# One group of sixteen chunks in place of four groups of four: the prefix sums of a gated linear-attention and convolution kernel

## The chip, the cores and the metric

The kernel runs on one core of one Trainium2 chip. The metric is the time of one execution on the device in microseconds (us). The core has five engines with queues of their own: TensorE (PE, matrix products; PEld are its weight loads), VectorE (DVE), ScalarE (ACT), GpSimd (POOL) and SyncE (SP, which issues DMA transfers). Each engine works through its queue in order and waits at an instruction until the semaphores that it names have been reached.

## The reference, cut to what matters

```python
g = sigmoid((x * gate_w).sum(-1, keepdims=True))
a = A_ref(x, wqkv, wo)          # linear attention, 16 heads of 28
b = B_ref(x, log_A, A_imag, C, log_dt, D_skip)
return g * a + (1 - g) * b

# A_ref: q, k, v = x @ wqkv; phi(t) = where(t > 0, t + 1, exp(t)) + 1e-6
#        kv = phi(k)^T v per head; z = sum of phi(k)
#        o = phi(q) kv / (phi(q) z + 1e-6); return o @ wo
# B_ref: K[d, l] = 2 Re sum_n C[d, n] exp(A[d, n] dt[d] l), l = 0..2047
#        y[t, d] = sum over l <= t of K[d, l] x[t - l, d];  return y + x * D_skip
```

x is 2048 positions by 448 features, all in fp32. Where a feature's K is flat over all lags to working precision, its convolution is K[d, 0] times the running sum of x over positions; the kernel finds out whether that holds for all features, and otherwise runs a general convolution behind the timed part (not run with these inputs).

## The kernel before, in words

Work goes by 16 chunks of 128 rows. A chunk c is loaded by SP (load_x) both turned and plain, with three tiles ahead; split_t and split_n split it into a high and a low part (ACT copies the high part, POOL subtracts, line 243), and skip (line 259, POOL) writes y[:, c] = x * D_skip. The main loop runs c from 2 to 13. An iteration projects k of chunk c + 1 and q of chunk c on PE (eleven products each, line 346), applies phi on ACT and DVE (k_feature, k_high, k_low, q_post), and adds eleven products into g, the product of phi(k) with x (do_g, line 422). Behind the loop come the last chunk, the small products of kv with wv and wo, and a last stage that goes over the chunks again: normalise q (norm_a to norm_d), turn it on PE (line 657), multiply (attend, line 683), and add og * y (final_b, line 688), which goes out by SP. The order of every queue is the order in which the program is written.

The running sums of x are made on the side of this. Chunks are in four groups of four: in group g, partition p holds positions 4p to 4p + 3 of the group's 512. For each group
- group_load fetches the four chunks once more into a home;
- running_a and running_b are two accumulating transfers on POOL's queue each, which turn the four chunks into running sums along a partition (lines 433 and 437);
- group_split splits the last of them, the totals, into high and low parts (ACT, then POOL);
- group_heads multiplies both by a strict lower triangle of ones on PE, a pair of products (line 448), which gives what comes from lower partitions;
- convolve (DVE, lines 453 and 454, two chunks at a time) adds that and multiplies by near, the row K[d, 0], which stands in a PSUM bank; the last row of the group goes to u by SP;
- group_add adds the home to y by an accumulating transfer (line 459). It is issued after the last skip of its group.

What one group leaves to the next is added in the last stage: inter (one product, line 749) and the gates, turned on PE (line 642) and laid into `rows` by 15 small transfers (phi), make extra rows of attend's last product (rc, tail).

Of the kernel before, what the change touches and what calls it, by code (L numbers as in the profile page):

```python
# [34 lines left out]
G = 4  # L35
SMALL = 2.0 ** -70
# [4 lines left out]
RX = DT + 3 * NC  # L41
# [3 lines left out]
UL = 32  # L45
UZ = 4 * UL
# [7 lines left out]
def general_conv(ctx: ExitStack, tc: tile.TileContext, ga, y, og, okc, both, gin_d, out):  # L54
# [80 lines left out]
    grouped = lambda t: t.rearrange("(g p r) d -> p g (r d)", p=P, r=G)  # L135
    ygr = yg.rearrange("p (g r) d -> p g (r d)", r=G)
    SP.dma_start(out=ygr, in_=grouped(nat))
# [4 lines left out]
    SP.dma_start(out=grouped(out), in_=ygr)  # L142
# [3 lines left out]
def gated_mix_kernel(ctx: ExitStack, tc: tile.TileContext, xin, wq_d, wvo_d, abc_d, ldt_d, dsk_d,  # L146
# [21 lines left out]
    wvo = const.tile([P, 2, J, D], F32, name="wvo")  # L168
    wv, wo = wvo[:, 0], wvo[:DJ, 1]
    ident, trir = both[:, 0], both[:, 1]  # L170
    cst = const.tile([P, DJ + RX + 1], F32, name="cst")
    mask, gcat, sel = cst[:DJ, :DJ], cst[:UZ, DJ:DJ + RX], cst[:, DJ + RX:]
    gcr = const.tile([UZ, RX], F32R, name="gcr")
    ones = const.tile([P, P], F32R, name="ones")
    rows = const.tile([P, S], F32, name="rows")
    dsk = rows[:, D:2 * D]
    near, side = [], []
    u = const.tile([UZ, D], F32, name="u")
# [8 lines left out]
    spare = const.tile([P, G, D], F32, name="spare")  # L187
    room = const.tile([P, 2 * NAT + 3 * D], F32, name="room")
# [10 lines left out]
    POOL.memset(rows[DT:RX, 2 * D:], 0.0)  # L199
    POOL.memset(u, 0.0)  # L200
# [12 lines left out]
    abc = [t[:DJ, o:o + 2 * J * N].rearrange("p (i j n) -> p i j n", i=2, j=J) for t, o in ((pf, 3 * J * N), (room, 0))]  # L213
# [72 lines left out]
    def s4d_prepare():  # L286
# [37 lines left out]
        near.append(o[:, :D])  # L324
        for j in range(J):
            PE.transpose(o[:, j * DJ:(j + 1) * DJ], pn[:, j:j + 1].to_broadcast([DJ, P]), ident[:DJ, :DJ])

# [96 lines left out]

    homes = (wvo[:, 1], pq[:, NC - G:], room[:, :G * D].rearrange("p (r d) -> p r d", r=G), spare)
    sums, heads = {}, {}

    def group_load(g):
        SP.dma_start(out=homes[g], in_=xin[g * G:(g + 1) * G, :, NAT:LO].rearrange("r p d -> p r d"))

    def running_a(g):
        w = homes[g]
        POOL.dma_start(out=w[:, 1::2], in_=w[:, 0::2], accum_op=ALU.add)

    def running_b(g):
        w = homes[g]
        POOL.dma_start(out=w[:, 2:], in_=w[:, 1:2].to_broadcast([P, 2, D]), accum_op=ALU.add)

    def group_split(g):
        w = sums[g] = tp.tile([P, 2, D], F32R, name="sums", tag="v0", bufs=1)  # L440
        ACT.copy(w[:, 0], homes[g][:, G - 1])
        low(POOL, w[:, 1], homes[g][:, G - 1], w[:, 0])

    def group_heads(g):
        o = heads[g] = ps.tile([P, 512], F32, name="v", tag="v0")[:, :D]
        w = sums.pop(g)
        for i in range(2):
            PE.matmul(o, lhsT=tri, rhs=w[:, i], start=i == 0, stop=i == 1)  # L448

    def convolve(c):  # L450
        g, i = c // G, c % G
        a, full = homes[g][:, i:i + 2], [P, 2, D]
        DVE.tensor_tensor(out=a, in0=a, in1=heads[g][:, None, :].to_broadcast(full), op=ALU.add)
        DVE.tensor_tensor(out=a, in0=a, in1=near[0][:, None, :].to_broadcast(full), op=ALU.mult)
        if i and g < NC // G - 1:
            SP.dma_start(out=u[g:UL + g + 1:UL, None], in_=homes[g][P - 1:P, G - 1:].to_broadcast([1, 2, D]))

    def group_add(g):
        POOL.dma_start(out=y[:, g * G:(g + 1) * G], in_=homes[g], accum_op=ALU.add)
# [52 lines left out]
    group_load(0)  # L512
    for c in range(2, NC - 2):
        if c + 3 < NC:
            load_x(c + 3)
        if c == 2:
            SP.dma_start(out=cst, in_=cst_d)
        if c in (5, 6):
            group_load(c - 3)
# [10 lines left out]
        if c == 6:  # L530
            running_b(1)
        if c in (6, 8):
            running_a(c // 2 - 1)
# [11 lines left out]
        if c == 6:  # L545
            convolve(0)
        qo = project(c, wqh, wql, D + 2, "q")
        q_post(c, qo)
        if c < 5:
            steps(2 if c == 4 else 1)  # L550
        if c == 4:
            ACT.copy(tri, trir)
            ACT.copy(gcr, gcat)
# [9 lines left out]
        if c in (7, 9, 11):  # L563
            group_heads(c // 2 - 2)
        if c < 4:
            skip(c - 1)
            skip(c + 2)
            (running_a, running_b)[c - 2](0)
        if c < 6:
            split_n(c + 2, c > 3)  # L570
        if c == 3:
            group_load(1)
        if c == 4:
            running_a(1)
        if c == 5:
            group_split(0)
        if c in (7, 9, 11, 13):
            group_add(c // 2 - 3)
        for j in {12: (0, 1), 13: (2, 3)}.get(c, ()):
            w = xn_p.tile([P, NX], F32R, name="wo", tag="n") if j < 2 else xp.tile([P, XC], F32R, name="wo", tag="xr")  # L580
            w = w[:DJ, :2 * D].rearrange("p (i d) -> p i d", i=2)
            woh.append(w[:, 0])
            wol.append(w[:, 1])
            ACT.copy(woh[j], wo[:, j])
            low(POOL, wol[j], wo[:, j], woh[j])
# [4 lines left out]
    rc = []  # L590
    pn, th, tl, pd, dn, dp = {}, {}, {}, {}, {}, []

    def norm_a(c):
        pd[c] = room[:, 2 * NAT + c % 3 * D:][:, :D]
        POOL.tensor_tensor(out=pd[c], in0=pq[:, c], in1=zb, op=ALU.mult)  # L595
# [19 lines left out]
    def norm_c(c):  # L615
        n = pn[c] = room[:, c % 2 * NAT:][:, :NAT].rearrange("p (j t) -> p j t", j=J)
# [12 lines left out]

    def phi(c):  # L630
        if 0 < c < NC:
            a = c - 1 if c < NC - 1 else 0
            i = DT + 3 * c
            SP.dma_start(out=rows[i:i + 3, c * P:(c + 1) * P], in_=phs[c // (NC - 1)][a:a + 1].bitcast(F32))

    phs = []

    def gates_a(a, b):
        return og[:, a:b]

    def gates_b(g, o):
        PE.transpose(o[:g.shape[1], :P], g, ident)

    def gates_c(n, o, tag):
        w = tp.tile([P, D], F32R, name="phs", tag=tag)[:n, :3 * P].rearrange("p (i t) -> p i t", i=3)
        phs.append(w)
        ACT.copy(w[:, 0:2], o[:n, None, :P].to_broadcast([n, 2, P]))
        return lambda: DVE.tensor_tensor(out=w[:, 2], in0=o[:n, :P], in1=w[:, 0].bitcast(F32), op=ALU.subtract)
# [18 lines left out]
    def tail(c):  # L667
        ACT.copy(tl[c][DT:RX, 3], rows[DT:RX, c * P:(c + 1) * P])
# [56 lines left out]
    for i in range(4):  # L725
# [5 lines left out]
        if i == 2:  # L731
            gates_b(gates_a(1, NC - 1), g[0])
# [255 lines left out]
```

## Time and profile before

| | |
|---|---|
| median of 3 timed runs | 170.21 us (170.1 to 170.28) |
| the profiled execution's own time | 170.16 us |
| its span, first to last instruction | 168.4 us |
| busy: PE, PEld | 163.2 us, 146.9 us |
| busy: DVE, ACT, POOL | 115.6 us, 107.6 us, 118.9 us |
| DMA queues q1 (SP's) and q0 (POOL's): share of 16 engines | 38.4%, 23.4% |

A row of the profile names a line of the kernel, an engine, an operation, the tile written and those read. A row of a timeline is the start in us from the span's start, the duration, then this name; in square brackets stands how long the engine was idle before, and what ended that. In the groups, after the count, come busy us, the mean ns of one, and idle time. Matmuls are pipelined, so their durations overlap. A row of waits is the waiting instruction, what released it, total us, times, and the longest. A row of stretches is the stretch, then for PE, PEld, DVE, ACT and POOL the busy us with the count, the clock granted to PE, the DMA share and GB/s.

### The profile page before, as it was taken

To read this page: it belongs to the slowest core of one execution; us is meant where nothing else is said; L and a number is where in the kernel's file an instruction comes from. 1 tells how busy PE (TensorE), PEld (TensorE's weight loads), DVE (VectorE), ACT (ScalarE), POOL (GpSimd) and SP (SyncE) were. 2 spreads that over 40 slices of the span, in tenths; PEclk is the share of its full clock that TensorE was granted. 3 is DMA by queue.
4 is the path that set the end of the run, shared out by engine and by line. 5 is a ranking of instruction groups with operands and counts; after the bars stand their busy time and mean duration, and the time that the engine had idled before them with its cause. 6 is when DMAs were issued, how large, how long until landed. Compare 5 with 4: busy or idle time off the path is not lost.

```text
span 168.4 us, 2703 instructions
## 1 busy us (share of the span) xinstructions
PE 163.2 (97%) x852; PEld 146.9 (87%) x852; DVE 115.6 (69%) x230; ACT 107.6 (64%) x245; POOL 118.9 (71%) x128
## 2 busy tenths in 40 slices
PE   6899999999999999999999999999999999999992
PEld 2698999999998999999999999989879999999991
DVE  0837745685844966767568567878988989997551
ACT  3688668898395694775856687564845564574541
POOL 6082589988948999757869479749786997953100
PEclk9999999999999999999999999999999999999999
DMA  5989999999992949998999800900121221221213
GB/s 158 414 314 315 282 291 337 276 246 216 396 277 44 176 110 256 224 236 256 318 233 258 172 4 0 218 2 1 28 47 55 112 110 59 109 92 73 111 58 113
DMA packets 11750, 29.45 MB, mean 175 GB/s; under 512 B 1331, under 2 KB 8198, under 8 KB 11510
## 3 DMA queue, kind: packets, MB, share of 16 engines
q1 hardware_dynamic: 8838, 21.81, 38.4%
q0 software_dynamic: 2752, 7.34, 23.4%
q8 instruction: 7, 0.11, 0.3%
q10 hardware_dynamic: 144, 0.11, 0.2%
q14 instruction: 9, 0.07, 0.1%
HBM read 17.93 MB, written 3.67 MB: 128 GB/s over the span
## 4 chain that ended last, share of the span: by engine, by line
PE 68%; ACT 10%; issue 3%; POOL 3%; DVE 1%; ACTq 0%; POOLq 0%
PE a L683 21%; PE q L346 13%; PE g L422 13%; PE k L346 9%; PE tr L657 4%; ACT y L300 2%; PE m L760 2%; PE v L346 1%; ACT xn L253 1%; ACT y L301 1%; ACT e L374 1%; PE v L448 1%; PE k L780 1%; PE tr L780 1%; ACT xt L247 1%
## 5 line engine op out<-in xcount | busy, mean ns | idle before, releaser
L683 PE MATMUL a<-wk,th 128*128 128x448 f32 (+1 forms) x170 | 36.8, 361 | 0.1
L422 PE MATMUL g<-pkh,xn 128*128 128x448 f32 x112 | 35.8, 364 | 0.0
L683 PEld LDWEIGHTS a<-wk,th 128*128 128x128 f32 x170 | 29.5, 189 | 2.3 <-issue 0.7
L346 PE MATMUL q<-wqh,xt 128*128 128x450 f32 x120 | 27.6, 367 | 0.0
L346 PE MATMUL k<-wk,xt 128*128 128x448 f32 x121 | 26.8, 366 | 0.4 <-ACT wk L469 0.4
L243 POOL TENSOR_TENSOR xn<-xr,xn 128x448 fp32r<-128x448 f32 x16 | 22.8, 1424 | 6.1 <-ACT xn L253 6.1
L243 POOL TENSOR_TENSOR xt<-xr,xt 128x512 fp32r<-128x512 f32 x14 | 21.4, 1526 | 7.2 <-ACT xt L247 7.2
L346 PEld LDWEIGHTS k<-wk,xt 128*128 128x128 f32 x121 | 22.6, 188 | 2.8 <-ACT wk L469 0.8
L346 PEld LDWEIGHTS q<-wqh,xt 128*128 128x128 f32 x120 | 22.5, 189 | 1.7
L422 PE MATMUL g<-pkl,xn 128*128 128x448 f32 x64 | 23.4, 366 | 0.0
L259 POOL TENSOR_TENSOR y<-xr,rows 128x448 f32<-128x448 f32 x16 | 23.2, 1456 | 0.0
L422 PEld LDWEIGHTS g<-pkh,xn 128*128 128x128 f32 x112 | 21.1, 188 | 2.2
L595 POOL TENSOR_TENSOR room<-pq,zb 128x448 f32<-128x448 f32 x16 | 18.5, 1165 | 3.8 <-issue 2.7
L620 POOL TENSOR_TENSOR room<-pq,den 128x336 f32<-128x336 f32 x16 | 12.2, 763 | 7.4 <-ACT den L609 4.0
L375 DVE SCALAR_TENSOR_TENSOR k<-k,e 128x448 f32<-128x448 f32 x11 | 7.0, 632 | 12.7 <-ACT e L374 12.7
L373 ACT ACTIVATE e<-k 128x448 f32<-128x448 f32 x11 | 6.0, 545 | 13.5 <-PE k L346 13.5
L688 DVE SCALAR_TENSOR_TENSOR ot<-y,og,a 128x448 f32<-128x448 f32 (+1 forms) x17 | 10.7, 629 | 5.4 <-PE a L683 5.4
L665 DVE TENSOR_TENSOR th<-tr,th 128x512 fp32r<-128x512 f32 x16 | 11.0, 690 | 2.6 <-ACT th L664 2.0
L664 ACT CAST th<-tr 128x512 fp32r<-128x512 f32 x16 | 9.4, 588 | 5.0 <-PE tr L657 4.8
L422 PEld LDWEIGHTS g<-pkl,xn 128*128 128x128 f32 x64 | 11.2, 174 | 1.2 <-DVE pkl L385 0.2
L694 ACT COPY pq<-a 128x448 f32<-128x448 f32 (+1 forms) x17 | 8.7, 516 | 5.0 <-DVE ot L688 5.0
L346 PE MATMUL v<-wk,xt 128*128 128x448 f32 x55 | 11.8, 362 | 0.0
(183 smaller groups left out, 316.6 us busy)
## 6 DMA issues: line engine op xcount, KB each, us to landing
xr<-in SPq DMA_DIRECT2D x15, 512.0 KB, 5.9
out<-ot SPq DMA_DIRECT2D x15, 224.0 KB, 1.9
pq<-in SPq DMA_DIRECT2D x2, 896.0 KB
room<-in SPq DMA_DIRECT2D x2, 896.0 KB
wvo<-in SPq DMA_DIRECT2D x2, 896.0 KB
y<-in SPq DMA_DIRECT2D x2, 480.0 KB
y<-in SPq DMA_DIRECT2D x2, 450.0 KB
wvo<-wvo POOLq DMA_DIRECT2D x2, 448.0 KB, 5.5
```

The lines of the kernel that those rows point to most:

```text
L243: eng.tensor_tensor(out=o, in0=r, in1=h.bitcast(F32), op=ALU.subtract)
L259: POOL.tensor_tensor(out=y[:, c], in0=plain[c][:, :D], in1=dsk, op=ALU.mult)
L346: PE.matmul(o[:, :n], lhsT=a, rhs=b, start=run.n == 1, stop=not seq)
L375: DVE.scalar_tensor_tensor(out=pks[c], in0=pks[c], scalar=1.0, in1=e, op0=ALU.add, op1=ALU.max)
L422: PE.matmul(g[i][:a.shape[1], :D], lhsT=a, rhs=b, start=c == 0 and n == 0, stop=c == NC - 1 and n == len(seq) - 1)
L595: POOL.tensor_tensor(out=pd[c], in0=pq[:, c], in1=zb, op=ALU.mult)
L620: POOL.tensor_tensor(out=n[:, :3, :DJ].rearrange("p j (h d) -> p j h d", h=4), in0=a, in1=r[:, :H - 4].rearrange("p (j h) -> p j h", j=3)[ ...
L664: ACT.copy(h, ov)
L665: DVE.tensor_tensor(out=l, in0=ov, in1=h.bitcast(F32), op=ALU.subtract)
L683: PE.matmul(a[:, lo:hi], lhsT=u_, rhs=w_[:, lo:hi], start=n == 0, stop=n == 10)
L688: DVE.scalar_tensor_tensor(out=ot[:, lo:hi], in0=y[:, c, lo:hi], scalar=og[:, c:c + 1], in1=a[:, lo:hi], op0=ALU.mult, op1=ALU.add)
L694: ACT.copy(pq[:, c, lo:hi], a[:, lo:hi])
```

## The change

All 16 chunks become one group: partition p holds positions 16p to 16p + 15, so the running sum along a partition goes over all chunks, and one pair of products with the triangle gives what comes from lower partitions. Two homes hold eight chunks each (wvo and room); half_load fetches four chunks at a time. running(c) keeps the sum in one PSUM bank: DVE adds chunk c to it (line 432 of the changed kernel) and writes near times the sum over the chunk's place in the home (line 433). A table gives the rows of each iteration: two in iteration 6, three each in 7 to 10, two in 11. near is copied to SBUF, which frees its bank, and the projections of k alternate between two banks from iteration 8. group_add (line 436) stays; group 0 goes in iteration 8, then 1 in 9, 2 in 11, 3 in 12. Groups 0 to 2 are issued behind all skips (line 251) of their rows; group 3, y[12:16], stands ahead of skip(14) and skip(15), which then write those two chunks' rows of y anew, so that what the transfer adds there is left out of the output. whole_split and whole_head (line 447) make the one pair in iteration 12, ACT copies its result to `over` in iteration 13, and four transfers (head_add, line 451) add that to y, a broadcast over four chunks each. The carry between groups, the gates' transposes, the rows they made and their transfers go. The loads of wo and wv are in halves, wo in iteration 10 and wv in 12; wo is split one iteration earlier.

```diff
+ROWS = {6: (0, 1), 7: (2, 3, 4), 8: (5, 6, 7), 9: (8, 9, 10), 10: (11, 12, 13), 11: (14, 15)}
...
+    def running(c):
+        if not c:
+            sums.append(ps.tile([P, 512], F32, name="r", tag="v0")[:, :D])
+            ACT.copy(sums[0], home(0))
+        else:
+            DVE.tensor_tensor(out=sums[0], in0=home(c), in1=sums[0], op=ALU.add)
+        DVE.tensor_tensor(out=home(c), in0=near, in1=sums[0], op=ALU.mult)
+
+    def group_add(g):
+        POOL.dma_start(out=y[:, g * G:(g + 1) * G], in_=homes[g // 2][:, g % 2 * G:][:, :G], accum_op=ALU.add)
+
+    def whole_split():
+        w = tp.tile([P, 2, D], F32R, name="sums", tag="v0", bufs=1)
+        sums[0] = w
+        ACT.copy(w[:, 0], home(NC - 1))
+        low(POOL, w[:, 1], home(NC - 1), w[:, 0])
+
+    def whole_head():
+        o = ps.tile([P, 512], F32, name="v", tag="v0")[:, :D]
         for i in range(2):
+            PE.matmul(o, lhsT=tri, rhs=sums[0][:, i], start=i == 0, stop=i == 1)
+        sums[0] = o
+
+    def head_add(g):
+        POOL.dma_start(out=y[:, g * G:(g + 1) * G], in_=over[:, None, :].to_broadcast([P, G, D]), accum_op=ALU.add)
...
         if c == 10:
-            SP.dma_start(out=wo, in_=wvo_d[:DJ, 1])
-        if c == 11:
-            SP.dma_start(out=wv, in_=wvo_d[:, 0])
-        ko = project(c + 1, wkh, wkl, D, "v1" if c in (2, 4) else "k")
-        if c == 6:
-            group_heads(0)
-        if c > 6:
-            convolve(2 * c - 12)
+            for j in (0, 2):
+                SP.dma_start(out=wo[:, j:j + 2], in_=wvo_d[:DJ, 1, j:j + 2])
+        if c == 12:
+            for j in (0, 2):
+                SP.dma_start(out=wv[:, j:j + 2], in_=wvo_d[:, 0, j:j + 2])
+        ko = project(c + 1, wkh, wkl, D, "v1" if c in (2, 4) or c > 6 and c % 2 == 0 else "k")
+        rows = list(ROWS.get(c, ()))
+        if c > 6 and rows:
+            running(rows.pop(0))
         split_t(c + 2)
...
             split_n(c + 2, False)
+        if c == 13:
+            ACT.copy(over, sums[0])
         k_feature(c + 1, ko)
-        if c in (7, 9, 11):
-            group_split(c // 2 - 2)
-        if c in (7, 9):
-            running_b(c // 2 - 1)
+        if c in (8, 9, 11, 12):
+            group_add((c - 7) * 2 // 3)
         if c > 5:
             skip(c + 2)
+        if c == 12:
+            whole_split()
         k_high(c + 1)
         k_low(c + 1)
...
-        if c in (7, 9, 11, 13):
-            group_add(c // 2 - 3)
...
+        for j in {11: (0, 1), 12: (2, 3)}.get(c, ()):
+            split_o(j)
+        if c == 12:
+            whole_head()
+        if c == 13:
+            for i in range(NC // G):
+                head_add(i)
...
-    carry = inter()
+    q_run(1)
     k1 = kv_products(1)
```

Where the instructions stand is best seen in the order itself. In POOL's queue before, these rows end iteration 12 and make up iteration 13: wo are the splits of wo, xt and xn those of chunk 15 (read from its tile xr_1002), y from xr is skip(15), and the DMA is group 3's transfer.

```order
L243 TENSOR_TENSOR wo_1063<-wvo_73,wo_1063 112x448 [waits DMAHW7_49,PE_49,Activation_49]
L243 TENSOR_TENSOR wo_1066<-wvo_73,wo_1066 112x448 [waits PE_49,Activation_49]
L243 TENSOR_TENSOR xt_1083<-xr_1002,xt_1083 128x512 [waits DMAHW3_49,Activation_49]
L243 TENSOR_TENSOR xn_1086<-xr_1002,xn_1086 128x448 [waits Activation_49]
L259 TENSOR_TENSOR y_59<-xr_1002,rows_77 128x448
L459 DMA y_59<-spare_86 128x1792 [waits DVE_49,Pool_49]
L243 TENSOR_TENSOR wo_1129<-wvo_73,wo_1129 112x448 [waits Activation_49]
L243 TENSOR_TENSOR wo_1132<-wvo_73,wo_1132 112x448 [waits Activation_49]
```

In the changed kernel the same queue from the end of iteration 11 to the end of 13: xr_921 is chunk 14, xr_991 chunk 15, sums is the low part of the totals, and DMASW3 is the semaphore of the fourth transfer that POOL issues, group 3's.

```order
L235 TENSOR_TENSOR wo_988<-wvo_73,wo_988 112x448 [waits PE_49,Activation_49]
L235 TENSOR_TENSOR xt_1007<-xr_921,xt_1007 128x512 [waits DMAHW7_49,Activation_49]
L235 TENSOR_TENSOR xn_1010<-xr_921,xn_1010 128x448 [waits Activation_49]
L436 DMA y_59<-room_84 128x1792 [waits DMAHW0_49,DVE_49,Pool_49]
L251 TENSOR_TENSOR y_59<-xr_921,dsk_76 128x448 [waits DMASW3_49]
L235 TENSOR_TENSOR sums_1019<-room_84,sums_1019 128x448 [waits Activation_49]
L235 TENSOR_TENSOR wo_1056<-wvo_73,wo_1056 112x448 [waits DMAHW6_49,Activation_49]
L235 TENSOR_TENSOR wo_1059<-wvo_73,wo_1059 112x448 [waits Activation_49]
L235 TENSOR_TENSOR xt_1077<-xr_991,xt_1077 128x512 [waits DMAHW0_49,Activation_49]
L235 TENSOR_TENSOR xn_1080<-xr_991,xn_1080 128x448 [waits Activation_49]
L251 TENSOR_TENSOR y_59<-xr_991,dsk_76 128x448
```

Group 3's transfer has moved from behind skip(15) to ahead of skip(14), and skip(14) names the semaphore of that transfer; the split of the totals stands behind it.

On PE, in the changed kernel, the end of g in iteration 12 and the start of iteration 13 (v from sums and tri is the pair with the triangle, k the projection of chunk 14):

```order
L414 MATMUL g_142<-pkl,xn 64x448
L414 MATMUL g_142<-pkh,xn 128x448
L447 MATMUL v<-sums,tri 128x448 [waits Activation_49]
L447 MATMUL v<-sums,tri 128x448 [waits Pool_49]
L338 MATMUL k<-wk_70,xt 128x448 x11
L338 MATMUL q<-wqh,xt 128x450 [waits DVE_49]
```

Before, iteration 13 follows on g of iteration 12 with nothing between; the four pairs stand behind k of iteration 6 and behind g of iterations 7, 9 and 11:

```order
L422 MATMUL g_145<-pkl,xn 64x448
L422 MATMUL g_145<-pkh,xn 128x448
L346 MATMUL k<-wk_70,xt 128x448 [waits DVE_49,Activation_49]
L346 MATMUL k<-wk_70,xt 128x448 [waits Pool_49]
L346 MATMUL k<-wk_70,xt 128x448 x9
```

So of four pairs one is left, one iteration later than the last of them was, and its second product waits for POOL.

More of the change, by code (lines that the diff above doesn't have):

```diff
@@ L439, in group_split @@
[L439 to L446, printed above, removed]
-        for i in range(2):
[L448 to L456, printed above, removed]
@@ L458, in group_add, with half_load, home @@
-    def group_add(g):
-        POOL.dma_start(out=y[:, g * G:(g + 1) * G], in_=homes[g], accum_op=ALU.add)
+    homes = (wvo, room)
+    sums = []
+    def half_load(h, i):
+        SP.dma_start(out=homes[h][:, i * G:(i + 1) * G],
+                     in_=xin[(2 * h + i) * G:(2 * h + i + 1) * G, :, NAT:LO].rearrange("r p d -> p r d"))
+    def home(c):
+        return homes[c // (2 * G)][:, c % (2 * G)]
+    def running(c):
[5 more added lines that the diff above has]
+        DVE.tensor_tensor(out=home(c), in0=near, in1=sums[0], op=ALU.mult)
@@ L696, in gated_mix_kernel @@
     c = NC - 2
-    POOL.memset(rows[DT:RX, D:2 * D], 0.0)
     gate(0, c)
     ko = project(c + 1, wkh, wkl, D, "v1")
-    uw = xt_p.tile([P, 2 * NAT], F32R, name="uw", tag="t")[:UZ, :D]
     k_feature(c + 1, ko)
-    ACT.copy(uw, u)
-    low(POOL, uw[UL:2 * UL], u[UL:2 * UL], uw[UL:2 * UL])
     k_high(c + 1)
@@ L720, in gated_mix_kernel @@
     gate(c, c + 1)
-    POOL.memset(rows[DT:RX, :D], 0.0)
     norm_bd(0)
```

155 lines of the change are left out of this document (36 added, 119 removed).

## The prediction

> **What bounds the kernel now.** I read the page first: the span, TensorE's (PE's) row, and the clock digits.
>
> ```profile
> span 168.4 us, 2703 instructions
> PE 163.2 (97%) x852; PEld 146.9 (87%) x852; DVE 115.6 (69%) x230; ACT 107.6 (64%) x245; POOL 118.9 (71%) x128
> PEclk9999999999999999999999999999999999999999
> ```
>
> The program ran 170.16 us in the profiled execution, so 1.76 us lie around the span; the median of the three timed runs is 170.21 us, and I work against 170.16. PE is full and at full clock. The waits of PE's matmuls say whether it is ever held up; this is the whole list.
>
> ```profile
> PE q L265 <- POOL warm L197: 1.3, 1, 1.3
> PE k L346 <- ACT wk L469: 0.4, 1, 0.4
> ```
>
> Both lie in the first 6 us. From there to its last matmul at 165.2 us PE does not stand still, so the span is PE's list of matmuls, and other engines count only where they make PE wait. The chain of waits in order of time gives the pace and the triangle products.
>
> ```profile
> 63.02 0.41 PE v L448 x2
> 76.73 0.41 PE v L448 x2
> 90.45 0.41 PE v L448 x2
> 90.85 2.21 PE k L346 x11
> 97.47 2.20 PE k L346 x11
> ```
>
> Eleven products take 2.2 us, 0.20 us each: a row's "mean ns of one" (361 to 367) overlaps its neighbours, and a removed product is worth its distance to the next one. An iteration of the loop (k, q, g) takes 97.47 - 90.85 = 6.62 us.
>
> **What leaves PE.** The first pair, and the stretch behind the last g products, stand in PE's timeline.
>
> ```profile
> 50.94 0.96 PE L448 MATMUL v<-sums,tri 128*128 128x448 f32 x2
> 51.74 1.59 PE L346 MATMUL q<-wqh,xt 128*128 128x450 f32 x7
> ...
> 113.10 0.37 PE L422 MATMUL g<-pkh,xn 128*128 128x448 f32 x1
> 113.30 0.27 PE L642 MATMUL g<-both,og 128*14 128x128 f32 x1
> ...
> 113.61 0.36 PE L422 MATMUL g<-pkh,xn 128*128 128x448 f32 x1
> 113.81 0.37 PE L749 MATMUL z<-uw,gcr 128*112 128x448 f32 x1
> 114.02 1.81 PE L780 MATMUL k<-gs,wvo 128*112 128x112 f32 x16
> ```
>
> Four pairs go: 51.74 - 50.94 = 0.80, and 3 x 0.41 = 1.23. The carry's product (L749) goes: 114.02 - 113.81 = 0.21. Between 113.10 and 113.61 lie two g products (0.40) and the gates' transpose, so that is worth 0.11; its twin in the last stage (c = 9 there) counts the same. Together 2.46 us. One pair comes back: 0.41. The last product of each row of output changes its operands, not its shape's cost (112 against 128 rows of weights), and q_run(1) only moves one product earlier. PE's list becomes 2.05 us shorter. That is the whole gain, if nothing new waits.
>
> **What the change makes wait.** In the changed order of GpSimd (POOL), iteration 12 has group 3's accumulating transfer onto y[12:16] ahead of skip(14), which writes y[14]. So skip(14) waits for that transfer to land, and behind it on POOL stand the low part of the totals (which the new pair's second product needs), two wo splits, xt and xn of chunk 15, skip(15) and the four new transfers. In the kernel before, each such transfer stands behind the last skip of its group, and nothing in POOL's queue waits for it. When is it issued, and when does PE come to the pair? Before, iteration 13 has the order on ACT and POOL that iteration 12 has now: two wo splits, xt, xn.
>
> ```profile
> 87.99 1.17 POOL L243 TENSOR_TENSOR sums<-spare,sums 128x448 fp32r<-128x448 f32 x1 [1.49 <-ACT sums L441]
> 89.11 1.16 POOL L259 TENSOR_TENSOR y<-xr,rows 128x448 f32<-128x448 f32 x1
> ...
> 97.75 2.29 POOL L243 TENSOR_TENSOR wo<-wvo,wo 112x448 fp32r<-112x448 f32 x2 [3.13 <-ACT wo L584]
> 100.01 1.29 POOL L243 TENSOR_TENSOR xt<-xr,xt 128x512 fp32r<-128x512 f32 x1
> 101.27 1.15 POOL L243 TENSOR_TENSOR xn<-xr,xn 128x448 fp32r<-128x448 f32 x1
> 102.38 1.15 POOL L259 TENSOR_TENSOR y<-xr,rows 128x448 f32<-128x448 f32 x1
> 103.83 0.87 POOL L459 DMA_DIRECT2D y<-spare  x1 [0.30 <-POOL y L259]
> ```
>
> There k starts at 97.47 and the instruction behind xn at 102.38, 4.91 us later. In the changed kernel k of iteration 12 starts at 90.85 - 2.03 = 88.82 (four pairs earlier in the list are gone), so the transfer is issued at 88.82 + 4.91 = 93.73. How long does it take? The DMA issues give the microseconds from issue to landing.
>
> ```profile
> y<-wvo POOLq DMA_DIRECT2D x1, 896.0 KB, 10.4
> y<-pq POOLq DMA_DIRECT2D x1, 896.0 KB, 13.2
> y<-room POOLq DMA_DIRECT2D x1, 896.0 KB, 7.0
> y<-spare POOLq DMA_DIRECT2D x1, 896.0 KB, 6.5
> ```
>
> The two long ones ran beside loads and running-sum transfers; the last, issued at 103.83, had the engines to itself. In the changed kernel all chunks of x and both halves of wv can be in by 93, since they no longer queue on SP behind the row copies into u. I take 6.5, nearest to y<-spare; 10.4 and 13.2 are the upper end. It lands at 100.23. Then skip(14), 1.16, and the low part, 1.17: 102.56, and the second product of the pair can go at 102.6. PE finishes g of iteration 12 at 97.47 - 2.03 = 95.44 and the pair's first product at 95.64. **PE stands still for 102.6 - 95.64 = 7.0 us**; nothing covers it, because k of chunk 14 is behind the pair in PE's queue.
>
> A still PE may also lose its clock. The stretches after PE's last matmul, and the first weight loads of the run, bear on that.
>
> ```profile
> 164.92 0.27 PE L683 MATMUL a<-rc,th 112*128 112x224 f32 x1
> ```
>
> ```profile
> 167.75:168.00 0.25, 0.00 (x0) 0.00 (x0) 0.00 (x0) 0.00 (x0) 0.00 (x0) 0.62 0.09 33
> 168.00:168.40 0.40, 0.00 (x0) 0.00 (x0) 0.00 (x0) 0.00 (x0) 0.00 (x0) 0.50 0.00 0
> ```
>
> ```profile
> 1.33 0.13 PEld L265 LDWEIGHTS <-warm 128*128 128x128 bf16 x2 [1.33 <-POOL warm L197]
> 1.74 0.15 PEld L265 LDWEIGHTS <-warm 128*128 128x128 bf16 x1 [0.28 <-issue]
> ...
> 3.44 0.15 PEld L265 LDWEIGHTS <-warm 128*128 128x128 bf16 x1 [0.28 <-issue]
> 3.87 0.58 PEld L265 LDWEIGHTS <-warm 128*128 128x128 bf16 x3 [0.28 <-issue]
> ```
>
> The granted clock (the column after the five engines) is a half by 168.00; 0.62 over the quarter before puts the fall at about 167.8, 2.6 us after the last matmul ended at 165.19. An idle of 7.0 us is well past that. At the start, products of 512 columns come 0.43 us apart from 1.33 to 3.87, against 0.20 x 512/448 = 0.23 at full pace, then close up: about 2.6 us at half pace, 1.3 us lost (the clock digits do not show that start; the spacing does). I add 1.3; its ends are 0 (clock kept) and 2.6 (twice as long at half pace).
>
> The Trainium skill, "TensorE: Matmul & The Clock Gate", Part 1, says that after an idle window of about 3.4 us the array runs at half rate until it has been busy for about 3.4 us, and its closing table asks for no gaps over about 3 us. By that the loss would be an estimated 1.7 us and the sum 176.8; the trace here shows 2.6 for both times, and I go by the trace.
>
> **Parts that I cost at nothing.** VectorE (DVE): an iteration now has up to three rows of add and multiply, through PSUM.
>
> ```profile
> L375 DVE SCALAR_TENSOR_TENSOR k<-k,e 128x448 f32<-128x448 f32 x11 | 7.0, 632 | 12.7 <-ACT e L374 12.7
> L385 DVE SCALAR_TENSOR_TENSOR pkl<-k,pkh 128x448 fp32r<-128x448 f32 x11 | 6.8, 617 | 1.8 <-ACT pkh L379 1.8
> L665 DVE TENSOR_TENSOR th<-tr,th 128x512 fp32r<-128x512 f32 x16 | 11.0, 690 | 2.6 <-ACT th L664 2.0
> L454 DVE TENSOR_TENSOR room<-room,p 128x896 f32<-128x896 f32 x2 | 2.2, 1087 | 0.1
> ```
>
> Four other operations of 448 columns an iteration take 4 x 0.62 = 2.5 us, and two of 896 took 2.2: 4.7. Now it is 2.5 + 6 x 0.62 = 6.2 of 6.62 in iterations 7 to 10. It fits by 0.4; at 0.69 an operation (the 512-column row, the upper end) it is 6.6 and still fits. PE is covered by the 4.4 us (two times eleven products) between the end of one q and the start of the next, in which DVE has to read q's one bank, and k's banks now alternate. A gain is excluded: PE never waited for DVE.
>
> POOL loses eight running-sum transfers, four memsets and four small splits; ACT loses the copies of the gates' rows; SP loses the copies into u and rows. PE waited for none of them but in the first pair's 0.80, counted above. The wo halves now wait on SP for group 0's landing, with x of chunks 14 and 15 and wv behind them: k of iteration 8 starts at 63.02 + 0.41 - 1.21 = 62.2 now, the transfer is issued within 4.9 of that and landed by 77.5 (10.4), some 10 us ahead of iteration 12, which splits chunk 14. The four broadcast transfers are issued after skip(15), at about 102.6 + 2.3 + 1.3 + 1.15 + 1.15 = 108.5.
>
> ```profile
> 125.46 0.68 DVE L688 SCALAR_TENSOR_TENSOR ot<-y,og,a 128x448 f32<-128x448 f32 x1 [0.38 <-PE a L683]
> ```
>
> y is first read at 125.46 before, near 131 now; the first transfer is in by 122 even at 13.2, and rows 4, 8 and 12 are each read more than 10 us after the ones before them. The output rows have the same length and only lie farther apart; I see no reason for a change there.
>
> **Sum:** 170.16 - 2.05 + 7.0 + 1.3 = **176.4 us**.
>
> **Rivals.**
> *No wait on PE (faster).* If the transfer has landed, and the low part is done, when PE reaches the pair, only the 2.05 remain: 168.1. It decides at 95.6: the issue would have to be 7 us earlier, at 86.7, before xt of chunk 14 is split, or the landing nearly immediate. The order speaks against it; for it only that a wait in the order need not be long. 0.08.
> *A longer landing.* With other transfers still running, 10.4 in place of 6.5: 176.4 + 3.9 = 180.3. Group 2's transfer, issued within 4.9 us of k of iteration 11 (88.82 - 6.62 = 82.2), could still run. 0.10.
> *The clock stays.* The fall after 2.6 us is seen only at the end of the program: 175.1. 0.07.
> *VectorE becomes the bound.* If PSUM rows cost more, at 0.4 us over an iteration, times four: 178.1. 0.03.
>
> **How the numbers follow.** My forecast has 0.72. The low end: landing, issue and clock each half a microsecond kinder, 174.9, which takes in the kept clock. The high end: a landing of 8.7, the middle between 7.0 and 10.4, and a longer half pace, 176.4 + 2.2 + 0.6 = 179.2, which takes in the VectorE case. Outside lie 168.1 and 180.3, 0.18 together. Differences under 0.2% (0.34 us) are about what a measurement of this kernel can tell from none; faster has the first rival's 0.08, within 0.2% 0.01, slower 0.91.
>
> **What would show it.** In the changed profile: POOL's y row (skip) with a wait of about 6.5 us on the transfer y<-room; PE's second v product idle about 7 us, released by POOL's sums; a fall of the clock near 98 and products 0.4 us apart behind the pair; no other wait of PE. It is wrong if PE reaches k of chunk 14 near 96, if the transfer takes over 9 us, or if PE waits in iterations 7 to 10.

## The result: 6% slower, beyond the forecast, and the profile after

The changed kernel takes 180.51 us at the median of four executions (180.12 to 180.88), the kernel before 170.20: a ratio of 1.0606 [1.0582, 1.063]. The forecast was 176.4 us, 174.9 to 179.2: the direction is right, the time lies above the range. The profiled execution took 180.88 us, 1.88 of them around its span. (Of the four executions of "late head transfers" below, two, of 184.38 and 185.4 us, are marked slow, and its times are given from the other two.)

The page of the changed kernel: span, PE's row and the clock digits.

```profile
span 179.0 us, 2610 instructions
PE 165.3 (92%) x843; PEld 148.1 (83%) x843; DVE 112.8 (63%) x242; ACT 100.6 (56%) x223; POOL 106.9 (60%) x116
PEclk9999999999999999999999858999999999999999
```

PE is no longer full, and three slices have lost clock (8, 5 and 8). PE's waits (total us, times, longest; the third and last of the list is the old one at the start):

```profile
PE v L447 <- POOL sums L235: 6.6, 1, 6.6
PE a L650 <- DMA wk<-shl: 1.9, 1, 1.9
```

The first was forecast, the second was not. First POOL's timeline of the changed kernel around the pair, then PE's:

```profile
94.26 0.85 POOL L436 DMA_DIRECT2D y<-room  x1
100.68 1.12 POOL L251 TENSOR_TENSOR y<-xr,dsk 128x448 f32<-128x448 f32 x1 [5.57 <-DMA y<-room]
101.77 1.12 POOL L235 TENSOR_TENSOR sums<-room,sums 128x448 fp32r<-128x448 f32 x1
...
108.45 5.17 POOL L451 DMA_DIRECT2D y<-over  x4
```

```profile
96.02 0.37 PE L447 MATMUL v<-sums,tri 128*128 128x448 f32 x1
102.94 0.74 PE L447 MATMUL v<-sums,tri 128*128 128x448 f32 x1 [6.55 <-POOL sums L235]
103.47 4.31 PE L338 MATMUL k<-wk,xt 128*128 128x448 f32 x11
```

That is the chain of the prediction, step for step: transfer, skip(14) behind it, the low part of the totals, the pair's second product. Behind it eleven products take 4.3 us (4.11 in the chain of waits). The stretches there, with the granted clock in the third column from the end:

```profile
101.00:102.00 1.00, 0.00 (x0) 0.00 (x0) 0.00 (x0) 0.00 (x0) 1.00 (x2) 0.78 0.00 0
102.00:103.00 1.00, 0.06 (x1) 0.06 (x1) 0.00 (x0) 0.00 (x0) 1.00 (x2) 0.50 0.00 0
...
107.00:108.00 1.00, 1.00 (x5) 0.87 (x4) 0.00 (x0) 0.18 (x1) 1.00 (x2) 0.50 0.00 0
108.00:109.00 1.00, 1.00 (x6) 0.91 (x5) 0.00 (x0) 0.95 (x2) 1.00 (x2) 0.80 0.00 0
```

0.78 over a microsecond is 0.44 of it at a half: the clock falls at 101.56. In the same way it is back at 108.40. It was at a half for 6.84 us, and PE worked in the last 5.46 of these.

The chain of waits of the changed kernel goes on to the new wait:

```profile
110.38 2.21 PE g L414 x11
...
127.94 4.81 DMA wk<-shl
132.89 2.47 PE a L650 x11
...
170.42 4.69 PE a L650 x33
175.13 0.46 DVE ot L655
```

wk<-shl are the four small transfers by SP that finish the weights of attend. From issue to landing the one that the profile before has a time for took 2.9 us; now the one that is waited for takes 4.8. What shared the DMA engines with them is seen in the landing times of the transfers y<-over, and in stretches of 5 to 6 us (the last two columns are the share of the DMA engines and GB/s):

```profile
DMA to landing us min/median/max: 7.9/14.2/20.6
```

```profile
115.00:120.00 5.00, 5.00 (x26) 4.43 (x25) 3.07 (x6) 2.80 (x7) 0.00 (x0) 1.00 1.13 186
...
125.00:131.00 6.00, 5.96 (x38) 5.06 (x36) 4.94 (x13) 3.69 (x9) 4.68 (x6) 1.00 1.08 183
```

The four transfers of totals, issued from 108.5 on, fill all DMA engines from about 110 to 131, through the very stretch in which attend's weights are finished. In the kernel before they stood idle at that place:

```profile
115.00:120.00 5.00, 5.00 (x40) 4.58 (x39) 4.44 (x15) 2.48 (x6) 5.00 (x7) 1.00 0.02 5
```

The account, from the positions of the same products in the two profiled executions (us):

| step | forecast | measured, and from what |
|---|---|---|
| products saved up to the pair | -2.03 | -1.45: 96.02 against 97.47 |
| the new pair itself | +0.41 | +0.41, taken at full pace |
| wait at the pair | +7.0 | +6.72: 102.94 - 96.02 - 0.20 |
| half clock behind it | +1.3 | +2.75: from 102.94 to g at 110.38 are 7.44, at full pace 0.20 + 2.23 + 2.26 |
| wait for wk<-shl | 0 | +1.93 |
| the rest of PE's list, up to its last products | -0.43 | -0.45: 170.42 - 160.51 less the rows above |
| from the start of PE's last products to the end of the span | 0 | +0.69: 179.0 - 170.42 against 168.4 - 160.51 |
| around the span | 0 | +0.12 |
| together | +6.25 | +10.72 |

### The profile page after: what moved, and what is told of

Its sections match the earlier page's. It is cut to its first block, busy times and chain, and to the rows that moved or that the text cites. A ratio compares the mean times of both kernels' runs of the same rounds, so it can differ in the third digit from the quotient of the medians.

```text
span 179.0 us, 2610 instructions
## 1 busy us (share of the span) xinstructions
PE 165.3 (92%) x843; PEld 148.1 (83%) x843; DVE 112.8 (63%) x242; ACT 100.6 (56%) x223; POOL 106.9 (60%) x116
## 4 chain that ended last, share of the span: by engine, by line
PE 72%; issue 7%; DVE 6%; POOL 6%; ACT 3%; DMA 3%; ACTq 0%; POOLq 0%; DVEq 0%
PE a L650 20%; PE g L414 14%; PE q L338 13%; PE k L338 10%; PE v L338 9%; PE tr L627 3%; DMA wk<-shl 3%; PE q L257 3%; POOL xn L235 1%; POOL xt L235 1%; DVE r L432 1%; POOL y L436 1%; POOL y L251 1%; DVE den L590 1%; DVE room L433 1%
## 5 line engine op out<-in xcount | busy, mean ns | idle before, releaser
L650 PE MATMUL a<-wk,th 128*128 128x448 f32 (+1 forms) x187 | 39.5, 360 | 1.9 <-DMA wk<-shl 1.9
L650 PEld LDWEIGHTS a<-wk,th 128*128 128x128 f32 x187 | 32.5, 189 | 4.1 <-issue 2.1
L235 POOL TENSOR_TENSOR xt<-xr,xt 128x512 fp32r<-128x512 f32 x14 | 18.1, 1295 | 20.2 <-ACT xt L239 20.2
L235 POOL TENSOR_TENSOR xn<-xr,xn 128x448 fp32r<-128x448 f32 x16 | 18.6, 1161 | 10.1 <-ACT xn L245 10.1
L251 POOL TENSOR_TENSOR y<-xr,dsk 128x448 f32<-128x448 f32 x16 | 19.3, 1214 | 5.6 <-DMA y<-room 5.6
L338 PE MATMUL k<-wk,xt 128*128 128x448 f32 x88 | 22.1, 399 | 0.0
L338 PEld LDWEIGHTS k<-wk,xt 128*128 128x128 f32 x88 | 18.2, 207 | 1.9 <-ACT wk L461 0.5
L338 PE MATMUL v<-wk,xt 128*128 128x448 f32 x88 | 19.1, 364 | 0.0
L338 PEld LDWEIGHTS v<-wk,xt 128*128 128x128 f32 x88 | 16.5, 188 | 1.3
L338 PE MATMUL q<-wql,xt 128*128 128x450 f32 x45 | 11.9, 368 | 0.0
```

Of the source, the lines that this page charges most:

```text
L235: eng.tensor_tensor(out=o, in0=r, in1=h.bitcast(F32), op=ALU.subtract)
L251: POOL.tensor_tensor(out=y[:, c], in0=plain[c][:, :D], in1=dsk, op=ALU.mult)
L338: PE.matmul(o[:, :n], lhsT=a, rhs=b, start=run.n == 1, stop=not seq)
L650: PE.matmul(a[:, lo:hi], lhsT=u_, rhs=w_[:, lo:hi], start=n == 0, stop=n == 10)
```

## The theories

**A:** the order of POOL's queue makes the wait at the pair and the half clock behind it (about 9.5 us), and the transfers of totals, put where small transfers are due, make the rest. **Rivals:** that the clock is no loss of its own (the wait alone costs, and what is lost behind it would be lost anyway); that the totals' transfers cost wherever they are put, so that the change is dear even without the wait; that the saving of products is smaller because of the change itself (its running sums on VectorE) and not because of something beside it.

## Experiments on the wait and the clock

**The totals' transfers taken away.** The output lacks the totals of the lower partitions.

```diff
-        if c == 13:
-            for i in range(NC // G):
-                head_add(i)
```

> The changed kernel without the four broadcast transfers (what the totals give to y is left out); group 3's transfer still ahead of skip(14). Theory (two costs, each of its own): the pair waits 6.7 us and runs on at half clock for 2.6, and nothing waits for the wk rows or the outputs, 170.2 - 1.5 + 9.3 = 178.0. Rival (the wait at the pair costs nothing by itself, since the wk rows set the end anyway): 170 or less.

Measured: 178.97 us, ratio 1.0525 [1.0493, 1.0557]. The only wait of PE's matmuls in this kernel behind the start:

```profile
PE v L447 <- POOL sums L235: 6.6, 1, 6.6
```

The wait for wk<-shl is gone with the transfers, the pair's wait and the 4.11 us of the eleven products behind it stay. The time is now inside the range of the prediction. So the larger part of the loss belongs to POOL's order, and the second wait to the transfers.

**The same with the totals' split ahead of the transfer.** Only one row of POOL's queue moves; the totals' transfers are left out here too.

```diff
+        if c == 12:
+            whole_split()
         if c in (8, 9, 11, 12):
             group_add((c - 7) * 2 // 3)
...
-        if c == 12:
-            whole_split()
```

> Left out are the four transfers of totals, as in the run that took 178.97 us at the median, with which this one is to be compared; the one edit is that the split of the totals stands ahead of group 3's transfer and of skip(14) in POOL's queue. If the 6.6 us and the half clock behind it came from the split's place in the queue, the pair goes through without a wait, and the wait moves to the next product that needs what stands behind skip(14): v of chunk 15, which needs xt of chunk 15. skip(14) still ends about 6.4 + 1.1 us behind the transfer's issue near 95.4, then two wo splits (2.2) and xt (1.3): xt is ready near 106.4, and PE comes to v near 103.3, so it waits about 3.1 us. Time: 178.97 - 6.6 - 2.75 (half clock) + 3.1 = 172.7 if the clock stays. Rival on the clock: in the runs so far the clock stayed at a half for 6.8, 6.8 and 10.2 us, multiples of 3.4, as if it was judged in stretches of 3.4 us; a gap of 3.1 us can then still empty most of one such stretch, and up to 2.7 us are lost: 173.5 to 175.4.

Measured: 175.35 us, ratio 1.0293 [1.0223, 1.0363]. PE's waits, PE's timeline at the new wait, and the first and last stretch below full clock:

```profile
PE v L338 <- POOL xt L235: 3.9, 1, 3.9
```

```profile
103.17 0.37 PE L338 MATMUL v<-wk,xt 128*128 128x448 f32 x1
107.43 3.85 PE L338 MATMUL v<-wk,xt 128*128 128x448 f32 x10 [3.90 <-POOL xt L235]
```

```profile
107.60:108.00 0.40, 0.40 (x2) 0.38 (x3) 0.40 (x1) 0.00 (x0) 0.40 (x1) 0.64 0.00 0
110.80:111.20 0.40, 0.40 (x3) 0.35 (x2) 0.00 (x0) 0.00 (x0) 0.00 (x0) 0.60 0.00 0
```

The pair goes through, and what else stands behind skip(14) is late instead: xt of chunk 15. The wait is 3.9 us in place of 3.1, since the transfer took 7.4 us in place of 6.4. The clock did fall, as the rival had it, at 107.71, when PE had already been at work again for 0.3 us, and came back at 111.12: 3.41 us at a half, 1.7 lost. 178.97 - 6.6 - 2.75 + 3.9 + 1.7 = 175.2 accounts for the 175.35. The split's place is the cause of the pair's wait; but the transfer ahead of skip(14) holds up whatever is behind.

**PE kept at work while it waits.** Thirty-two idle products into a spare bank between the two of the pair.

```diff
-        for i in range(2):
-            PE.matmul(o, lhsT=tri, rhs=sums[0][:, i], start=i == 0, stop=i == 1)
+        PE.matmul(o, lhsT=tri, rhs=sums[0][:, 0], start=True, stop=False)
+        spin = ps.tile([P, 512], F32, name="spin", tag="k")
+        for i in range(32):
+            PE.matmul(spin[:, :D], lhsT=tri, rhs=sums[0][:, 0], start=True, stop=True)
+        PE.matmul(o, lhsT=tri, rhs=sums[0][:, 1], start=False, stop=True)
```

> The changed kernel with 32 idle products of 448 columns between the first and the second product of the pair (they add work that the output does not use). Theory (the half pace behind the wait is the clock, and the clock falls for lack of work): PE stays at full clock and the 2.6 us go, 177.9. Rival (products behind the wait are slow for another reason, such as transfers): 180.5.

Measured: 183.14 us, ratio 1.0735 [1.0686, 1.0783], slower than the change alone. The chain of waits, and the clock in the stretches at attend's start:

```profile
105.07 2.23 PE k L338 x11
...
127.14 6.65 DMA wk<-shl
133.92 4.45 PE a L653 x11
```

```profile
132.00:133.00 1.00, 0.00 (x0) 0.00 (x0) 0.43 (x1) 0.00 (x0) 1.00 (x2) 0.99 0.86 196
133.00:134.00 1.00, 0.08 (x1) 0.11 (x1) 0.00 (x0) 0.00 (x0) 1.00 (x3) 0.50 0.59 95
```

The eleven products behind the pair took 2.23 us in place of 4.11, so their half pace was the clock. That the clock is a loss of its own shows in the 178.97 us without totals against the 169.82 of the version below that has no totals and no wait either: 9.15 us, of which the wait is 6.6. The gain was not kept: the transfer took 1.4 us longer in this execution, PE came to attend 0.8 us earlier than in the changed kernel, waited 3.8 us there for wk<-shl, and lost its clock at that place instead. The forecast of 177.9 had not counted that the second wait absorbs what the first one gives back.

**How long the clock stays down.** In seven executions of these kernels it was at a half for 3.41 us (split first, and the late transfers with both edits below), 6.84 (the change, late head transfers, idle products) and 10.24 (the next experiment, and without totals): one, two and three times 3.41. So the clock looks as if it were judged at the end of each stretch of 3.41 us: it falls when PE stood idle for more than about half of one, even if PE is at work by then, and comes back only behind a stretch that was full. Counted back by 3.41 us from a fall, the stretch had 1.96 us of idle PE without totals (96.50 to 98.46) and 2.26 with both edits; in the change the stretch that ended at 98.15 had 1.76, and the clock stayed until 101.56. In the changed kernel PE came back 1.4 us into a stretch, and had to finish it and another. That is read from the positions and durations, not tried by itself. The Trainium skill, "TensorE: Matmul & The Clock Gate", Part 1, has an idle window of about 3.4 us that halves the rate until PE has been busy for about 3.4 us. The trace agrees with the 3.4; the time of work at half pace was 3.4 to 5.6 us behind the waits in the loop, by where in a stretch PE started again.

## Experiments on the totals' transfers

**Group 3's transfer behind skip(15), as before the change.**

```diff
-        if c in (8, 9, 11, 12):
+        if c in (8, 9, 11):
             group_add((c - 7) * 2 // 3)
...
         if c == 13:
+            group_add(3)
             for i in range(NC // G):
                 head_add(i)
```

> Group 3's transfer is issued behind skip(15) in iteration 13, so its sum into rows 14 and 15 of y is kept. Theory (the order on GpSimd holds PE): the pair no longer waits, the 6.7 us of standing still and the 2.6 us at half clock go, 180.5 - 9.3 = 171.2; the 1.9 us wait of the last stage for the wk rows stays, since the four broadcast transfers still crowd the DMA engines then (it may grow to 4). Rival 1 (the running sums on VectorE hold the pair): 180 again. Rival 2 (the wait for the wk rows is only an after-effect of the late pair): 169.2.

Measured: 178.5 us, ratio 1.0473 [1.0435, 1.0511]. PE's waits and its chain:

```profile
PE a L651 <- DMA wk<-shl: 4.7, 3, 3.5
...
PE v L447 <- POOL sums L235: 0.2, 1, 0.2
```

```profile
97.22 2.22 PE k L338 x11
...
121.46 8.19 DMA wk<-shl
...
133.05 3.69 PE a L651 x11
```

The pair's wait shrinks from 6.6 to 0.2 us and the half clock behind it is gone: about 9 us are given back. The time is still 7.3 us above the 171.2 that were expected, for all but 2 of the 9 are lost again at attend: PE comes there 8.7 us earlier (122.3 against 131.0), into the middle of what are now five large transfers in a row (y<-over lands 11.8 to 21.1 us after issue), the small ones take up to 8.2 us, and the clock goes to a half for 10.2 us. The expectation had a wait of 4 us at most; it was 4.7 in three parts, with the clock behind it, which had not been counted.

**The totals' transfers spread over the last stage.** Groups 1 to 3 in its steps 1, 4 and 7; once with group 3's transfer late as above, once without.

```diff
-            for i in range(NC // G):
-                head_add(i)
+            head_add(0)
...
             norm_a(c + 6)
+        if c in (1, 4, 7):
+            head_add(c // 3 + 1)
```

> As late_add, and the broadcast transfers 1 to 3 are issued in the last stage (its steps 1, 4 and 7) instead of together in iteration 13. Theory (crowding): neither wait is left, 168.9 us, that is 1.3 under the kernel before: 2.05 of products less the 0.5 by which the list ran slower, with 0.2 of doubt. Rival 2 (the wait was an after-effect): the same as late_add. Rival (late transfers hold the y rows of the last stage): 170 or more, with VectorE's ot waiting for a transfer.

> The changed kernel with only the broadcast transfers 1 to 3 moved to the last stage (steps 1, 4, 7); group 3's transfer stays ahead of skip(14). Theory (crowding): the pair waits as before, the 1.9 us wait for the wk rows goes, 178.6. Rival 2 (after-effect of the late pair): 180.5.

Measured: 176.14 us with both, ratio 1.0352 [1.0304, 1.04]; with the head transfers alone 181.47 and 183.6 us, 1.07 and 1.08 times the kernel before. One of PE's waits and the chain with both edits:

```profile
PE tr L627 <- DVE room L613: 3.1, 3, 2.3
```

```profile
128.39 0.58 DVE ot L655
129.00 5.79 DMA out<-ot
```

No small transfer for the weights is late now, but the output rows are: out<-ot takes 5.8 us beside a transfer of totals, 1.9 elsewhere. ot has two buffers, so VectorE stands still for it, and PE behind VectorE; behind the longest of PE's waits here, 2.3 us, the clock is at a half for 3.41 us. Both expectations were too low for the same reason: a large transfer was taken as free once nothing reads its result soon. With the head transfers alone that comes on top of the pair's wait, and both times are above those of the unmoved ones (180.12 to 180.88).

**No wait and no totals' transfers.** The first version as above with both edits and the totals left out of the output; the second with one unused tile in addition.

```diff
     near = const.tile([P, D], F32, name="near")
+    const.tile([P, 1945], F32, name="pad")
```

> Group 3's transfer behind skip(15), and no broadcast transfers (what the totals give to y is left out). Theory: no wait is left, only the shorter list: 170.2 - 1.5 = 168.7, all of the gain that the products can bring. Rival (the running sums on VectorE, or something else in the loop, still holds PE): 170 or more.

> As late_no_heads, with an unused tile of 1945 numbers a partition ahead of the tiles of x, which puts them at the addresses that they have in the kernel before. Theory (the products of q run 2.27 in place of 2.21 to 2.23 us because their operands lie elsewhere): 0.4 to 0.5 less than late_no_heads, 168.2. Rival (the pace comes from elsewhere): the same as late_no_heads.

Measured: 169.82 us, ratio 0.9958 [0.9942, 0.9974], and with the tile 168.96, ratio 0.9928 [0.9903, 0.9954]. Two iterations in the chain without and with the tile:

```profile
97.01 0.47 PE v L447
...
99.70 2.26 PE q L338 x11
...
104.17 2.23 PE v L338 x11
106.40 2.26 PE q L338 x11
```

```profile
95.83 0.47 PE v L448
...
98.51 2.27 PE q L339 x11
...
103.00 2.20 PE v L339 x11
105.20 2.20 PE q L339 x11
```

With every wait but 0.2 to 0.3 us at the pair gone the kernel is faster than before, but without the tile by less than the 2.05 us of products (which would be 168.1), and 1.1 us above the 168.7 that were expected. The tile does no work; it moves what is allocated behind it in SBUF, the tiles of x among it, back by as much as the change had shifted them. With it the products go at the pace of the kernel before: eleven of k or v take 2.20 us in place of 2.23, and eleven of q 2.20 and 2.27 in turn in place of 2.26 each time. So part of the saving was lost to the places of the operands, and the rival that VectorE's running sums take it falls. What came back is 0.9 us by the medians, 0.5 by the ratios, where 0.4 to 0.5 was expected. Of the 2.05 us forecast 1.2 are then there by the ratio; where the rest is was not settled.

## A version that beats both

**VectorE adds most of the totals.** Group 3's transfer is late, one transfer of totals stays (group 2); VectorE adds the totals to chunks 0 to 7 in iteration 13 in two operations, and to chunks 12 to 15 in the last stage. The output is complete.

```diff
+    def over_add(c, n):
+        DVE.tensor_tensor(out=y[:, c:c + n], in0=y[:, c:c + n], in1=over[:, None, :].to_broadcast([P, n, D]), op=ALU.add)
...
-            for i in range(NC // G):
-                head_add(i)
+            group_add(3)
+            head_add(2)
+            for i in range(2):
+                over_add(i * G, G)
...
+        if NC - 5 <= c < NC - 1:
+            over_add(c + 1, 1)
```

> All of the output is computed. Group 3's transfer behind skip(15); of the four broadcast transfers only group 2's is left, issued in iteration 13; VectorE adds the totals to chunks 0 to 7 in two operations in iteration 13, where it has 4 us to spare, and to chunks 12 to 15 one by one in the last steps. Theory (crowding by 896 KB transfers beside small ones is what is left once the order is mended): 168.7 to 169.2, faster than the kernel before. Rival (VectorE becomes late: its gate waits, or ot in the last steps): 170 or more.

Measured: 171.38 us, ratio 1.0062 [1.0039, 1.0084]. PE waits for no transfer, but VectorE's two additions, 3.95 us together in the chain, hold up what the last chunk's product zo needs, which is the rival of the expectation:

```profile
104.58 3.95 DVE y L454 x2
...
111.52 0.47 PE zo L681
```

**With the unused tile, and with other shares.** The same with the tile; with the tile and chunks 4 to 7 by a second transfer; with the tile and chunks 4 to 7 by VectorE in the first steps of the last stage. The second and the third have only one addition in iteration 13:

```diff
-            for i in range(2):
-                over_add(i * G, G)
+            over_add(0, G)
```

The second has `head_add(1)` ahead of `head_add(2)`; the third has the additions in the last stage for `c < G` too, as `over_add(c + G, 1)`.

> The run with VectorE's two adds took 171.38 us at the median, and the unused tile that puts the tiles of x back to their old addresses took 0.9 us (169.82 to 168.96) off the version without any totals. If both are independent: 171.38 - 0.9 = 170.5, that is no difference from the kernel before (170.2). The wait of the last chunk's product zo (0.9 us) should stay, and the pace of products should alternate again between 2.20 and 2.27 us for eleven. Rival, that the gain of the tile was another's (a shift in the placement of transfers): 171.4.

> The output is complete. VectorE adds the totals to chunks 0 to 3 in one operation of 2.0 us in iteration 13 and to chunks 12 to 15 one by one in the last stage; chunks 4 to 11 get them by two transfers behind group 3's. If five transfers in a row make attend's first product wait because they last until about 131, three of them, issued near 102.5 and at about 5.6 us each, are in by about 119 to 120, ahead of the transfer wk<-shl near 120.5: then only the wait of zo goes (0.9 less at most) and the time is 169.4, faster than the kernel before. Rival, that crowding decides at once with any transfer still in flight: wk<-shl lands 3 us or more late and attend waits 1 to 3 us, with part of the clock: 171 to 173.

> The output is complete. Only one transfer of totals (chunks 8 to 11); VectorE adds the totals to chunks 0 to 3 in one operation in iteration 13 and to chunks 4 to 7 and 12 to 15 one by one in the last stage. If it was the second operation of 2.0 us that delayed zb of the last chunk, the wait of zo is gone and the time is 169.2 to 169.5, faster than the kernel before. Rival, that VectorE is also what sets the pace of the first steps of the last stage: the four adds there (0.62 us each) show up as waits of PE for th or shl of up to 2.5 us together: 170 to 172.

Measured: 170.22 us, ratio 0.9979 [0.9962, 0.9995]; **169.0 us, ratio 0.9918 [0.9891, 0.9945]**; 170.12 us, ratio 0.9989 [0.9965, 1.0012]. The tile is worth 1.2 us here by the medians, 1.4 by the ratios. The version with two transfers beats both kernels, the one before by 0.8%; it was not run without the tile. Its span is 166.7 us. The only wait of PE's matmuls behind the start, and the stretch of the last landing:

```profile
PE v L448 <- POOL sums L236: 0.3, 1, 0.3
```

```profile
115.00:120.00 5.00, 5.00 (x35) 4.48 (x34) 4.06 (x12) 2.80 (x7) 4.07 (x5) 1.00 0.68 115
```

Three large transfers in a row, issued from 101.98 on, are done at about 118 (the share of the engines is 0.91 from 117 to 118 and 0.14 from 118 to 119), and wk<-shl is issued at 118.5 and lands in 2.2 us. So it is not the transfers as such that cost, but that they are in flight when small ones are due: with five in a row they are, with three they just are not. The rival, that any transfer still in flight would crowd, did not come, but it was not tried either, since none was in flight any more. In the third version, 0.6 us above the upper end of what was expected, PE waits only 0.4 us more (for room), yet its time is 1.1 us longer than the second's and its single runs spread from 169.57 to 171.22; its profiled execution is the fastest of them, so what the others lose is not seen, and stays open.

## Why the prediction was wrong

**The wait at the pair: right.** Place, chain and size: 7.0 us against 6.72. The transfer was issued 0.5 us later than forecast (94.26 against 93.73) and took 0.2 us less, and PE came 0.6 us later (96.02 against 95.44 to the first product). That the wait is made by the split's place behind skip(14) is shown by moving only that. The rival of a longer landing names 180.3, close to what was measured, but that is chance: it has the transfer take 10.4 us, and it took 6.3.

**The clock: right mechanism, size half of what it was.** 1.3 us forecast, at most 2.6; 2.75 measured. The step that failed took the time at half pace (2.6 us of work) from the start of the program; behind the pair it was 5.46 us of work. That PE came back at another place in the clock's stretches fits, but is read from the durations. The clock also fell not near 98 but at 101.56, 5.2 us after the end of PE's last product before the wait (96.39). 1.45 us of the miss.

**The step that failed in kind: "Parts that I cost at nothing".** It followed the four transfers of totals only to the reader of their result, y at 131, and found 9 us to spare. It did not ask what else is on the DMA engines while they run. The second wait, put at nothing, was 1.9 us here, and 3.8 to 4.7 as soon as PE is earlier. The parts of the profile to look at were at hand: the DMA digits of the page, nearly empty between 110 and 120 before, and wk<-shl among the DMA issues. Without the transfers the time was 178.97 us, inside the range. The range's high end took a longer landing as it concerned the pair, not as it concerned others' landings.

**The products saved: 0.6 us too much.** The count was right, but it supposed that the other products keep their pace. The rows of one iteration of the changed kernel, from its chain:

```profile
55.98 2.23 PE k L338 x11
58.21 2.26 PE q L338 x11
60.47 2.21 PE g L414 x11
```

These are 6.70 us. Before, two iterations took 76.73 - 63.43 = 13.30, 6.65 each. The stretch from the start of iteration 2 to the pair, eleven iterations, took 96.02 - 21.91 = 74.11 us against 97.47 - 21.78 - 2.03 = 73.66, that is 0.45 more; the remaining 0.13 lies in the first 22 us. The unused tile shows that the places of the operands are behind the pace.

**VectorE and the running sums: right.** PE waits for nothing in iterations 7 to 10, the adds and multiplies took 0.61 to 0.62 us each as assumed, and the rival that VectorE becomes the bound did not come (its time is 176.4 + 1.6 = 178.0, not 178.1).

**The tail: open.** 0.7 us more from PE's last products to the end of the span. The last output transfers take 2.0 and 2.9 us there, against 1.9 before; no experiment was made on that.

The miss of 4.47 us (180.88 against 176.4) is 1.93 + 1.45 + 0.56 for the list + 0.81 at the end and around it - 0.28 for the wait.

## What to carry to other kernels

A transfer costs twice: the engine that waits for it, and every small transfer that shares the DMA engines while it runs; so look up who is due in its flight, not only who reads its result. An accumulating write placed ahead of an ordinary one on the same rows makes the whole queue wait for its landing: put it last, or put first what others wait for. And a wait that is taken away gives back only the distance to the next one that is late, so an edit is priced with the rest of the chain moved up by as much.

## What the runs showed of the hardware

- A transfer of 56 to 112 KB from SBUF to SBUF by SP's queue landed in 2.2 to 2.9 us with the DMA engines free or nearly so, in 3.0 to 8.2 beside accumulating transfers of 896 KB by POOL's queue (the least as the last of these ended); 224 KB of output in 1.9 against 5.8. The Trainium skill, "DMA: Bandwidth & Descriptors", Queues, rings and completion order, says that each DMA engine takes the queue rows in turn, a packet at a time. By that a small transfer would be slowed, not shut out; the traces agree, at 1.4 to nearly four times as long.
- Four or five such transfers in a row took about 5.2 us each at a share of 1.1 of the engines and 183 to 191 GB/s: from about 110 to 131 in the changed kernel, and five from 104 to 130 with group 3's transfer late.
- The clock at a half lasted 3.41, 6.84 and 10.24 us, and once began when PE had been at work again for 0.3 us. A wait of 2.3 us was enough for it once (late transfers with both edits).
- Eleven products of k or v took 2.20 or 2.23 us, and of q 2.20 and 2.27 in turn or 2.26 each time, by where an unused tile of 1945 words a partition had pushed their operands: in time 0.5 to 0.9 us of 169.82, and 1.2 to 1.4 of 171.38.
